# Two exponentials of the odd attention head side by side, with one shift of both row minima

## The chip, the core and the metric

The kernel runs on one core of a Trainium2 chip. A core has a matrix engine (TensorE, PE in the profile, with its weight loads shown apart as PEld), a vector engine (VectorE, DVE), an engine for activation functions (ScalarE, ACT), a general engine (GpSimd, POOL), and SyncE (SP), which here issues the transfers. Each engine works through its own list of instructions; semaphores make one wait for another. Matrix products go into PSUM, a small memory of banks, from which ACT and DVE read them. The metric is the device time of one run in microseconds (us).

## The reference

Two independent layers work on sequences of 2048 rows and 576 features, and their outputs stand side by side. The first is attention with a compressive memory: 32 heads of 18 features, in 4 segments of 512 rows.

```python
for s in range(N):
    qs, ks, vs = q[:, :, s], k[:, :, s], v[:, :, s]
    logits = jnp.einsum("bhqd,bhkd->bhqk", qs, ks) * scale + mask
    p = _softmax(logits, axis=-1)
    a_dot = jnp.einsum("bhqk,bhkd->bhqd", p, vs)
    ...
    o = g * a_mem + (1.0 - g) * a_dot
```

The mask is causal, so a block of 128 query rows needs 128, 256, 384 or 512 key columns. Ahead of the attention stand the projections of q, k and v, and behind it the output projection. The second layer is a Fourier mixing, `y = dft_seq_re @ a - dft_seq_im @ b` with `a` and `b` from two products over the features: large products with nothing to wait for but their operands.

## The kernel before

The program has three stretches: projections and memory sums; then attention, with the products of the Fourier layer ("dense work") as filler between its steps; then the rest of the dense work and the output projection. The edit touches the middle one, from about 245 to 905 us.

Its order is written out by hand. `attention()` is a generator that walks over pairs of heads, `p` from 0 to 67; each pair has eight slots, and after each slot it yields a weight. The driver (lines 1230 to 1239) then issues dense products until their share of the work has caught up. Operations given to `later` are issued so many slots after the call. Each engine gets its instructions in the order of this walk.

A pair of heads is in flight over several steps of `p`. The even head is worked with keys on the partitions (`t_fill`, banks with the tag `t`); the odd head with queries on the partitions (`f_fill`, `f_exp`), two steps later (`F_LAG = 2`). For the odd head:

- `f_fill(n, kind)` has PE compute scores into a PSUM bank (line 969), and DVE find each row's minimum of the negated, masked scores (`smallest`, line 975), into a column of the small tile `nb`. The four query blocks are dealt out to three banks by `ROWS`: kind 0 is the block with 512 columns (`nb` column 3), kind 1 those with 128 and 384 (columns 0 and 2), kind 2 the one with 256 (column 1). DVE's result appears in the profile as the row that reads its accumulator out.
- `f_exp(n, kind)` shifts these minima by a constant with an ACT copy (line 995), and then runs one exponential for each block of this kind on ACT (line 998), with the shifted minimum as its bias, from PSUM into the tile `pf`. After it the bank is free.
- `f_split_hi` (line 1005, ACT) and `f_split_lo` (line 1009, POOL and DVE) cut `pf` into a float16 pair `hl`; `f_turn` (line 1014) transposes that by a DMA from SP's queue, and `pv` (lines 1093 and 1094, PE) multiplies it by the values, a step later.

The banks: kinds 1 and 2 of the odd head share two banks, tag `s`, in turn with the three score steps `s_fill` of another even head (lines 969 and 975 again). `s_fill(n, 1)` in slot 1 takes the bank that kind 2 of the odd head used in slot 6 of the step before. Kind 0 goes to one of two `t` banks, which `t_fill(n, 1)` (line 1049, behind the small transpose of line 1026) takes next. In slot 4 the odd head's kind 0 takes this bank again, after DVE's `t_lo(n, 1)` (line 1076, `plo<-t`) has read the even head's exponentials, which line 1061 writes back into it.

Slots that matter, with what the edit touches: slot 3 to 4 has `f_fill` kinds 1 and 0; slot 6 has `pv` of another odd head, `f_fill` kind 2, `f_exp` kind 1; slot 7, the last, has `f_exp` kind 0 and `pv_out`; slot 0 of the next step has `t_lo`, `f_exp` kind 2 and `f_split_hi`; slot 1 has `s_fill` kinds 0 and 1 with `t_fill` kinds 0 and 1. Between slots, ACT also copies finished dense tiles out of PSUM (line 635 and line 652) and cuts the streamed DFT matrix into a high part (line 452), whose low part POOL makes (line 457).

Of the kernel before, what the change touches and what calls it, by code (L numbers as in the profile page):

```python
# [16 lines left out]
AF = mybir.ActivationFunctionType  # L17
# [6 lines left out]
P = 128  # L24
# [16 lines left out]
def infini_attention_and_fnet(ctx: ExitStack, tc: tile.TileContext, xT, wqk, w8, wv, wo, beta, xtT, cT, hT, out):  # L41
    nc = tc.nc
    act, dve, pool, pe = nc.scalar, nc.vector, nc.gpsimd, nc.tensor
# [44 lines left out]
    def later(n, fn, *a):  # L88
        due.setdefault(clock[0] + n, []).append((fn, a))
# [374 lines left out]
    def stacks(p_, i):  # L464
        qs_bufs.append(p_.tile([P, 4, L], BF16, name=f"qs{i}"))
        ks_bufs.append(p_.tile([P, 4, L], BF16, name=f"ks{i}"))
        pool.memset(ks_bufs[i].bitcast(F32)[96:], BF16_ONES)
# [20 lines left out]
    def stack_load(G):  # L488
        if G < NG:
            s, g8 = divmod(G, 8)  # L490
            rows = slice(g8 * 72, g8 * 72 + 72)
            for n, (buf, src) in enumerate(((ks_bufs, kd), (qs_bufs, qd))):
                later(1 + n, dma, buf[G % 4][:NPAIR], src[s][rows].rearrange("(h d) c t -> (d c) h t", d=DH))
# [71 lines left out]
    def bank(name, shape, dtype, tag):  # L565
        turns[tag] ^= 1
        return ps.tile(shape, dtype, name=name, tag=f"{tag}{turns[tag]}", bufs=1)
# [392 lines left out]
    ROWS = (((3, 0),), ((0, 384), (2, 0)), ((1, 0),))  # L960
    FIRST_COL = {3: 0, 2: 512, 0: 896, 1: 1024}
# [26 lines left out]
        smallest(o, kind, -SCALE, F_[n][0])  # L988
        F_[n][2][kind] = o

    def f_exp(n, kind):
        nb, f, o = F_[n]
        o = o.pop(kind)
        m = nb[:, (slice(3, 4), slice(0, 3, 2), slice(1, 2))[kind]]
        act.activation(m, m, AF.Copy, bias=LIFT)
        for i, c in ROWS[kind]:
            w = (i + 1) * P
            act.activation(f[:, FIRST_COL[i]:FIRST_COL[i] + w], o[:, c:c + w], AF.Exp, bias=nb[:, i:i + 1], scale=-1.0)  # L998

    def f_split_hi(n):  # L1000
        f = F_[n][1]
# [14 lines left out]
    def maxima(G):  # L1016
        m, b = NEGM[G % 2].rearrange("p (h n) -> p h n", h=2), MB[G % 2][:, :24].rearrange("p (h c n) -> p c h n", h=2, c=3)
        r = sa.tile([P, 2, 4], F32, name="negx", bufs=2)
        pool.tensor_copy(b[:, 0], m)
        pool.tensor_tensor(r, m, b[:, 0], OP.subtract)  # L1020
        pool.tensor_copy(b[:, 1], r)
        pool.tensor_tensor(b[:, 2], r, b[:, 1], OP.subtract)

    def maxima_transpose(G, o):
        t = o[:, 384:512]
        pe.matmul(t, MB[G % 2], ident16, start=True, stop=True)
        yield
        w = sa.tile([24, P], BF16, name="mt", bufs=2)
        act.activation(w, t[:24], AF.Copy)
        for h in range(2):  # L1030
            later(1, dma, qs_bufs[G % 4][NPAIR:NPAIR + 3, 2 * h].rearrange("c (n t) -> c n t", n=4), w[12 * h:12 * h + 12])
# [64 lines left out]
    def pv_out(n2):  # L1096
        G, hh = divmod(n2, 2)
        s, g8 = divmod(G, 8)
        o = PV.pop(n2)
        og = OG[G % 2]  # L1100
        h0 = 4 * g8 + 2 * hh
        w = o[:, 440:].rearrange("p (h i c) -> p h i c", h=2, c=1)
        b = o[:, :144].rearrange("p (h i d) -> p h i d", h=2, i=4)
        o = o[:, :440].rearrange("p (h i c) -> p h i c", h=2, i=4)
        a = sa.tile([P, 8, DH], F32, name="pa", bufs=2)
        dve.reciprocal(w, o[:, :, :, 54:])
        dve.tensor_tensor(w, w, g1[:, h0:h0 + 2, None, None].to_broadcast([P, 2, 4, 1]), OP.mult)
        dve.tensor_reduce(a, o[:, :, :, :54].rearrange("p h i (c d) -> p (h i) d c", c=3), axis=AX, op=OP.add)
        to = og[:, :, 36 * hh:36 * hh + 36].rearrange("p i (h d) -> p h i d", d=DH)
        a = a.rearrange("p (h i) d -> p h i d", h=2)  # L1110
        if s == 0:
            dve.tensor_tensor(to, a, w.to_broadcast([P, 2, 4, DH]), OP.mult)
        else:
            dve.tensor_tensor(b, a, w.to_broadcast([P, 2, 4, DH]), OP.mult)
            dve.tensor_tensor(to, to, b, OP.add)
        if hh == 1:
            later(6, turn_out, G)
# [33 lines left out]
    F_LAG, T_LAG, V_LAG = 2, 3, 4  # L1151
# [3 lines left out]
    def attention():  # L1155
        for p in range(NP + V_LAG):
            def even(lag, fn, *a):
                if 0 <= p - lag < NP:
                    fn(2 * (p - lag), *a)

            def odd(lag, fn, *a):
                if 0 <= p - lag < NP:
                    fn(2 * (p - lag) + 1, *a)

            if p < 2:
                OG.append(sa.tile([P, 4, 72], F32, name=f"og{p}"))
            if p == 0:
                stack_load(1)
                later(20, value_load, 0)
            if p % 2 == 0:  # L1170
                later(39, value_load, p // 2 + 1)
                later(30, memory_load, p // 2)
            even(T_LAG + 1, t_lo, 0)
            odd(F_LAG + 1, f_exp, 2)
            odd(F_LAG + 1, f_split_hi)
            yield SLOTS[0]
            G = p // 2 - 1 if p % 2 == 0 and 0 < p <= NP else None
            even(0, s_fill, 0)
            even(T_LAG, t_fill, 0)
            even(T_LAG, t_fill, 1, G)  # L1180
            even(0, s_fill, 1)
            if G is not None and p < T_LAG:
                list(maxima_transpose(G, bank("trm", [P, L], F32, "t")))
            odd(F_LAG + 1, f_split_lo, pool, 512, 1280)
            yield SLOTS[1]
            even(T_LAG, t_lo, 1)
            odd(F_LAG + 1, f_split_lo, dve, 0, 512)
            yield SLOTS[2]
            even(V_LAG, pv)
            if p < 2:  # L1190
                stacks(sq, p + 2)
            even(0, s_fill, 2)
            even(T_LAG, t_mask)
            yield SLOTS[3]
            odd(F_LAG, f_fill, 1)
            even(T_LAG, t_fill, 2)
            odd(F_LAG, f_fill, 0)
            if p % 2 and p < NP:
                maxima(p // 2)
            yield SLOTS[4]  # L1200
            odd(F_LAG + 1, f_turn)
            if p % 2:
                if p == 1:
                    later(6, stack_load, 2)
                else:
                    stack_load((p + 3) // 2)
                if 2 < p < 18:
                    later(2, copy_parts, 2, 7 + p // 2)
            elif 4 <= p < 36:
                later(2, copy_parts, 3, (p - 4) // 2)  # L1210
            even(T_LAG, t_hi)
            yield SLOTS[5]
            odd(V_LAG, pv)
            odd(F_LAG, f_fill, 2)
            odd(F_LAG, f_exp, 1)
            even(T_LAG, t_lo, 2)
            yield SLOTS[6]
            odd(F_LAG, f_exp, 0)
            if V_LAG <= p < NP + V_LAG - 1:
                pv_out(p - V_LAG)  # L1220
            yield SLOTS[7]
# [8 lines left out]
    for n, w in enumerate(attention()):  # L1230
        tick()
        ta += w
        for fn, a in PLAN.pop(n, ()):
            fn(*a)
        while td / total_d < ta / total_a:
            t = next(d, BREAK)
            if t is BREAK:
                break
            td += t
# [56 lines left out]
```

## Time and profile before

| | |
|---|---|
| median of 3 runs | 984.33 us (983.99 to 985.59) |
| the profiled execution's own time | 983.87 us |
| its span, first to last instruction | 982.2 us |
| granted PE clock, share of full | 0.999 |
| ACT copies of line 995 | x192, 38.0 us |
| ACT exponentials of line 998 | x256, 128.1 us |
| ACT halves of line 1005 | x128, 87.4 us |

The span is the time between the first and the last instruction of one profiled execution; that execution took 1.7 us longer in all. A row of the timeline gives the start, the duration, the engine, the line, the operation, the tile written and those read, shapes, and in brackets the idle time of the engine just before with what ended it. Rows of neighbours of one kind are merged (x2, x4). A table of stretches gives each engine's busy time between two moments; a table of waits says who waited for whom, in us, how often, and the longest. "PEld" rows are weight loads that run beside the products. A PE row's end is modelled, its start is not.

### The profile page before, as it was taken

How to read it: one execution, taken by the hardware profiler on the slowest of the kernel's cores; microseconds unless marked ns; L12 is line 12 of the kernel's file. 1: busy time of each engine (PE TensorE's matmuls, PEld its weight loads, DVE VectorE, ACT ScalarE, POOL GpSimd, SP SyncE). 2: the span in 40 equal slices, each digit the busy share in tenths (PEclk: the TensorE clock that was granted, in tenths of full speed). 3: DMA queues.
4: the chain of work that ended last, by engine and by line, in shares of the span. 5: the costliest groups of instructions: out<-in, count | busy, mean ns of one | idle time of the engine just before them, and what ended most of it. 6: DMA issues, size and time to landing. Idle time of an engine off the chain costs nothing.

```text
span 982.2 us, 25421 instructions
## 1 busy us (share of the span) xinstructions
PE 974.7 (99%) x9246; PEld 916.3 (93%) x9246; DVE 746.6 (76%) x2113; ACT 715.2 (73%) x1687; POOL 664.4 (68%) x746
## 2 busy tenths in 40 slices
PE   9999999999999999999999999999999999999998
PEld 8989989899999999999999999999999999999998
DVE  6657668594677767777887777778888899988884
ACT  6757576664887787877878788887777877878442
POOL 2657577686667766676776776667677987776561
PEclk9999999999999999999999999999999999999999
DMA  7637557766877998999999997789999999997663
GB/s 240 200 118 242 199 171 252 238 239 182 191 183 209 219 239 233 216 210 254 233 243 241 235 210 191 184 203 217 242 238 252 242 237 240 233 207 184 173 203 109
DMA packets 304350, 209.96 MB, mean 214 GB/s; under 512 B 204992, under 2 KB 259136, under 8 KB 304192
## 3 DMA queue, kind: packets, MB, share of 16 engines
q1 hardware_dynamic: 304000, 208.20, 82.5%
q8 instruction: 72, 1.18, 0.5%
q14 instruction: 54, 0.44, 0.1%
q10 hardware_dynamic: 224, 0.14, 0.0%
HBM read 122.37 MB, written 58.98 MB: 185 GB/s over the span
## 4 chain that ended last, share of the span: by engine, by line
PE 98%; ACT 1%; DVE 1%; issue 0%
PE d L584 41%; PE s L969 7%; PE v L84 6%; PE qk L84 6%; PE qk L251 6%; PE pv L1093 4%; PE d L629 3%; PE d L630 3%; PE d L631 3%; PE t L869 2%; PE pv L1094 2%; PE d L869 2%; PE s L869 2%; PE m L364 1%; PE t L1044 1%; PE look L397 1%
## 5 line engine op out<-in xcount | busy, mean ns | idle before, releaser
L975 DVE CUSTOM_DVE_ANT_0 s<-s,causal 128x128 f32<-128x128 f32 (+3 forms) x512 | 250.1, 504 | 104.3 <-PE s L969 98.1
L457 POOL TENSOR_TENSOR clo<-craw,chi 128x512 fp32r<-128x512 f32 x159 | 217.6, 1369 | 97.1 <-ACT chi L452 72.2
L584 PE MATMUL d<-wide,chi 128*128 128x288 f32 x1408 | 260.1, 302 | 0.0
L584 PEld LDWEIGHTS d<-wide,chi 128*128 128x128 f32 x1408 | 210.5, 188 | 0.7
L584 PE MATMUL d<-wide,clo 128*128 128x288 f32 x704 | 171.2, 310 | 0.0
L1009 POOL TENSOR_TENSOR hl<-pf,hl 128x768 f16<-128x768 f32 x64 | 113.9, 1780 | 70.3 <-ACT hl L1005 56.1
L969 PE MATMUL s<-ks,qs 108*128 108x128 bf16 (+3 forms) x512 | 131.6, 301 | 1.9 <-ACT pf L998 1.8
L1057 ACT ACTIVATE phi<-t 128x384 f16<-128x384 f32 x128 | 61.7, 482 | 98.1 <-PE t L1054 98.1
L998 ACT ACTIVATE pf<-s,nb 128x128 f32<-128x128 f32 (+3 forms) x256 | 128.1, 526 | 6.2
L584 PE MATMUL d<-ab,chi 128*128 128x288 f32 x640 | 122.3, 300 | 0.0
L584 PEld LDWEIGHTS d<-wide,clo 128*128 128x128 f32 x704 | 117.7, 188 | 0.9
L452 ACT ACTIVATE chi<-craw 128x512 fp32r<-128x512 f32 x160 | 99.6, 623 | 2.8 <-DMA craw<-xtT 1.8
L584 PEld LDWEIGHTS d<-ab,chi 128*128 128x128 f32 x640 | 97.6, 188 | 0.3
L1005 ACT ACTIVATE hl<-pf 128x768 f16<-128x768 f32 (+1 forms) x128 | 87.4, 729 | 2.0
L584 PE MATMUL d<-ab,clo 128*128 128x288 f32 x320 | 82.4, 306 | 0.0
L629 PE MATMUL d<-wide,chi 128*128 128x288 f32 x256 | 79.7, 311 | 0.0
L630 PE MATMUL d<-wide,chi 128*128 128x288 f32 x256 | 75.6, 295 | 0.0
L631 PE MATMUL d<-wide,clo 128*128 128x288 f32 x256 | 75.6, 295 | 0.0
L1061 ACT ACTIVATE pf<-t 128x512 f32<-128x512 f32 (+1 forms) x128 | 68.7, 537 | 7.4 <-PE t L1044 7.3
L1076 POOL TENSOR_TENSOR plo<-pf,phi 128x384 f16<-128x384 f32 x64 | 60.7, 948 | 15.1 <-ACT pf L1061 12.6
L969 PEld LDWEIGHTS <-qs 108*128 108x128 bf16 x512 | 44.4, 97 | 16.3 <-issue 2.7
L289 POOL TENSOR_TENSOR p<-r,p 128x512 bf16<-128x512 f32 x36 | 43.4, 1206 | 22.3 <-ACT p L288 21.1
(286 smaller groups left out, 2596.6 us busy)
## 6 DMA issues: line engine op xcount, KB each, us to landing
craw<-cT SPq DMA_DIRECT2D x128, 256.0 KB
ks<-kd SPq DMA_DIRECT2D x32, 432.0 KB
qs<-qd SPq DMA_DIRECT2D x32, 432.0 KB
craw<-xtT SPq DMA_DIRECT2D x32, 320.0 KB
vd<-vs SPq DMA_DIRECT2D x16, 440.0 KB
vst<-vd SPq DMA_DIRECT2D x32, 220.0 KB
qd<-p SPq DMA_DIRECT2D x16, 384.0 KB
kd<-p SPq DMA_DIRECT2D x16, 384.0 KB
```

What stands on the lines that cost most here:

```text
L84: pe.matmul(o, a, b, start=n == 0, stop=n == len(terms) - 1)
L452: act.activation(hi, raw[:, :4], AF.Copy)
L457: engine.tensor_tensor(lo, raw[:, :4], hi.bitcast(F32), OP.subtract)
L584: pe.matmul(o[h], a, b[:, h * 288:h * 288 + 288], start=start, stop=stop)
L629: pe.matmul(o, xh[:, k], wl[k][:, cs], start=k == 0, stop=False)
L630: pe.matmul(o, xh[:, k], wh[k][:, cs], start=False, stop=False)
L631: pe.matmul(o, xl[:, k], wh[k][:, cs], start=False, stop=False)
L969: pe.matmul(o[:, c:c + w], q[:, i * P:w], k[:, :w], start=True, stop=True)
L975: dve.tensor_tensor_reduce(o[:, c:c + w], o[:, c:c + w], CAUSAL[0][:, L - w:], scale=scale, scalar=-LOWEST, op0=OP.add, op1=OP.min, accum_ ...
L998: act.activation(f[:, FIRST_COL[i]:FIRST_COL[i] + w], o[:, c:c + w], AF.Exp, bias=nb[:, i:i + 1], scale=-1.0)
L1005: act.activation(hl[:, 0, a:b], f[:, a:b], AF.Copy)
L1009: engine.tensor_tensor(hl[:, 1, a:b], f[:, a:b], hl[:, 0, a:b], OP.subtract)
```

## The change

`f_exp` takes several kinds. It now shifts the minima of all of them with one copy over a strided slice of `nb`: columns 0 and 2 for kind 1, as before, and columns 1 and 3 for kinds 0 and 2 together. Then it runs the exponentials of the kinds in turn. Kind 2 leaves slot 0 of the following step; kinds 0 and 2 are done by one call in slot 7, the 512-column exponential first and the 256-column one behind it. The exponentials themselves, their operands and their banks stay as they are.

```diff
-    def f_exp(n, kind):
+    def f_exp(n, *kinds):
         nb, f, o = F_[n]
-        o = o.pop(kind)
-        m = nb[:, (slice(3, 4), slice(0, 3, 2), slice(1, 2))[kind]]
+        m = nb[:, 1 - kinds[0]::2]
         act.activation(m, m, AF.Copy, bias=LIFT)
-        for i, c in ROWS[kind]:
-            w = (i + 1) * P
-            act.activation(f[:, FIRST_COL[i]:FIRST_COL[i] + w], o[:, c:c + w], AF.Exp, bias=nb[:, i:i + 1], scale=-1.0)
+        for kind in kinds:
+            for i, c in ROWS[kind]:
+                w = (i + 1) * P
+                act.activation(f[:, FIRST_COL[i]:FIRST_COL[i] + w], o[kind][:, c:c + w], AF.Exp, bias=nb[:, i:i + 1],
+                               scale=-1.0)
+            del o[kind]
...
             even(T_LAG + 1, t_lo, 0)
-            odd(F_LAG + 1, f_exp, 2)
             odd(F_LAG + 1, f_split_hi)
             yield SLOTS[0]
...
             yield SLOTS[6]
-            odd(F_LAG, f_exp, 0)
+            odd(F_LAG, f_exp, 0, 2)
```

## The prediction

> **What bounds the kernel now.** First the page's first and fourth parts: busy time of each engine, and the chain that ended last.
>
> ```profile
> PE 974.7 (99%) x9246; PEld 916.3 (93%) x9246; DVE 746.6 (76%) x2113; ACT 715.2 (73%) x1687; POOL 664.4 (68%) x746
> PE 98%; ACT 1%; DVE 1%; issue 0%
> ```
>
> TensorE (PE) sets the end; the engine that the edit touches, ScalarE (ACT), has a quarter of its time free. So ACT's work counts only where PE waits for it. The second view is the table of stretches for the 660 us in which attention runs, the third the table of waits, cut to PE.
>
> ```profile
> 245.00:905.00 660.00, 658.04 (x7100) 621.28 (x7099) 527.15 (x1640) 527.11 (x1255) 468.40 (x524) 1.00 0.94 222
> PE s L969 <- ACT pf L998: 1.8, 4, 0.5
> ```
>
> Columns of the first row after the length: PE, PEld, DVE, ACT, POOL busy, clock, DMA share, GB/s. PE lacks 2 us of 660, and four waits for line 998, the exponentials of the odd head, are 1.8 us of them. A busy share can hide stalls, since ends of matmuls are modelled, so the starts are read in the timeline:
>
> ```profile
> 505.27 0.69 PE L584 MATMUL d<-wide,chi 128*128 128x288 f32 x4
> 505.79 0.43 PE L584 MATMUL d<-wide,clo 128*128 128x288 f32 x2
> ```
>
> Four products start in 0.52 us: 0.13 us each, closely packed. The Trainium skill (Perfetto Trace Analysis, Identifying the Most-Contended Engine) says that matmul busy time is a poor measure of the room left and that weight loading is a better one; by it some 7% would be open, and ACT's relief might buy more than four waits. The starts just quoted do not bear that out here.
>
> Fourth, the timeline at the first of the four waits:
>
> ```profile
> 257.92 0.69 ACT L998 ACTIVATE pf<-s,nb 128x512 f32<-128x512 f32 x1
> 258.54 0.41 ACT L635 ACTIVATE wide<-d 128x288 fp32r<-128x288 f32 x1
> 258.85 0.33 PE L1049 MATMUL t<-qs,ks 111*128 111x384 bf16 x1
> 259.07 0.47 ACT L998 ACTIVATE pf<-s,nb 128x256 f32<-128x256 f32 x1
> 259.60 0.38 PE L969 MATMUL s<-ks,qs 108*128 108x128 bf16 x2 [0.42 <-ACT pf L998]
> ```
>
> PE's score product at 259.60 needs the bank that the 256-column exponential frees at 259.54. That one stands behind an evacuation of a dense product (L635), emitted between the end of one pair and the start of the next. Its cost is read from starts: undisturbed, the score product follows L1049 after 0.16 us.
>
> ```profile
> 500.43 0.33 PE L1049 MATMUL t<-qs,ks 111*128 111x384 bf16 x1
> 500.59 0.38 PE L969 MATMUL s<-ks,qs 108*128 108x128 bf16 x2
> ...
> 283.57 0.33 PE L1049 MATMUL t<-qs,ks 111*128 111x384 bf16 x1
> 284.31 0.38 PE L969 MATMUL s<-ks,qs 108*128 108x128 bf16 x2 [0.42 <-ACT pf L998]
> ...
> 376.49 0.33 PE L1049 MATMUL t<-qs,ks 111*128 111x384 bf16 x1
> 377.30 0.38 PE L969 MATMUL s<-ks,qs 108*128 108x128 bf16 x2 [0.48 <-ACT pf L998]
> ...
> 447.71 0.33 PE L1049 MATMUL t<-qs,ks 111*128 111x384 bf16 x1
> 448.55 0.38 PE L969 MATMUL s<-ks,qs 108*128 108x128 bf16 x2 [0.51 <-ACT pf L998]
> ```
>
> The four distances are 0.75, 0.74, 0.81 and 0.84 us; less 0.16 each that is 0.59 + 0.58 + 0.65 + 0.68 = 2.50 us, all that PE loses to the banks of these exponentials (more than the 1.8 us of the waits, which count only from L1049's modelled end).
>
> **The change part by part.** *Removed:* one shift copy in each of 64 pairs, 0.20 us each (the row at 506.94 below), so 64 x 0.2 = 12.8 us of ACT. It lies under PE's work and is worth nothing in itself; without that cover it would be worth those 12.8 us.
>
> *Moved:* the 256-column exponential now starts right behind the 512-column one. Nothing is issued with it, no DMA moves, and PE's order stays as it is. At the other place in the loop, in an undisturbed pair:
>
> ```profile
> 506.94 0.20 ACT L995 ACTIVATE nb<-nb 128x1 f32<-128x1 f32 x1
> 507.17 0.69 ACT L998 ACTIVATE pf<-s,nb 128x512 f32<-128x512 f32 x1
> 507.25 0.14 DVE L975 DVE_READ_ACCUMULATOR2_ANT nb<- 128x1 f32 x1
> 507.76 0.62 ACT L452 ACTIVATE chi<-craw 128x512 fp32r<-128x512 f32 x1
> 508.50 0.47 ACT L998 ACTIVATE pf<-s,nb 128x256 f32<-128x256 f32 x1
> ```
>
> The next ACT instruction starts 0.59 us after a 512-column exponential (507.17 to 507.76), and the 256-column one takes 0.47: 1.06 us from the start of the first to the end of the second. In the four stalled pairs this ends at 257.92 + 1.06 = 258.98, against PE's undisturbed 259.01: the stall goes.
>
> ```profile
> 282.45 0.69 ACT L998 ACTIVATE pf<-s,nb 128x512 f32<-128x512 f32 x1
> 374.13 0.69 ACT L998 ACTIVATE pf<-s,nb 128x512 f32<-128x512 f32 x1
> 446.92 0.69 ACT L998 ACTIVATE pf<-s,nb 128x512 f32<-128x512 f32 x1
> ```
>
> Likewise 283.51 against 283.73 (gone); 375.19, even with a hold of 0.5 us as worked out below, against 376.65 (gone); and 447.98 against 447.87, which leaves 0.11 and some 0.05 for the release (ACT ended at 259.54, PE went at 259.60). With 0.03 left at the first, 2.50 - 0.16 - 0.03 = **2.3 us gained**.
>
> *Added:* the copy now waits for the 256-column minimum too. In the pair above that is read out at 507.25 + 0.14 = 507.39, so the copy starts near 507.42 in place of 506.94: ACT, which works in order, is held 0.48 us, and behind the copy stand the 512-column exponential, the cut of the next DFT chunk (L452), and the float16 halves (L1005). The second exponential still ends at 507.42 + 0.23 + 1.06 = 508.71, before its old 508.97. Read in this way in all 64 pairs the hold runs from none (the first pair) over 0.7 us (the last) to 1.54 us:
>
> ```profile
> 245.72 0.14 DVE L975 DVE_READ_ACCUMULATOR2_ANT nb<- 128x1 f32 x1
> 245.95 0.19 ACT L995 ACTIVATE nb<-nb 128x1 f32<-128x1 f32 x1
> ...
> 852.76 0.20 ACT L995 ACTIVATE nb<-nb 128x1 f32<-128x1 f32 x1
> 854.13 0.14 DVE L975 DVE_READ_ACCUMULATOR2_ANT nb<- 128x1 f32 x1
> ...
> 903.12 0.20 ACT L995 ACTIVATE nb<-nb 128x1 f32<-128x1 f32 x1
> 903.68 0.14 DVE L975 DVE_READ_ACCUMULATOR2_ANT nb<- 128x1 f32 x1
> ```
>
> Who waits behind it on PE? In the worst pair (852.76) the 512-column exponential ends at 854.30 + 0.24 + 0.69 = 855.23 and the 256-column one at 855.60; PE asks for their banks some 0.8 us later:
>
> ```profile
> 856.43 0.33 PE L1049 MATMUL t<-qs,ks 111*128 111x384 bf16 x1
> 856.59 0.38 PE L969 MATMUL s<-ks,qs 108*128 108x128 bf16 x2
> ...
> 857.49 0.50 ACT L1061 ACTIVATE t<-t 128x384 f32<-128x384 f32 x1
> 858.57 0.54 DVE L1076 TENSOR_TENSOR plo<-t,phi 128x384 f16<-128x384 f32 x1
> 860.51 0.38 PE L969 MATMUL s<-ks,qs 108*128 108x512 bf16 x1
> ```
>
> What is late next is the even head's chain: ACT's third exponential (L1061 into t), VectorE's (DVE's) difference (L1076), and the bank that PE needs for the odd head's 512 columns (L969). The hold moves ACT by about 1.3 us here (1.54, less the saved copy), the exponential's end from 857.99 to 859.3 and the difference to 859.9; PE comes at 860.51, so 0.6 us remain even here. After that ACT stands idle in any case until PE's next even scores, which takes the lateness away before the next pair:
>
> ```profile
> ACT phi L1057 <- PE t L1054: 98.1, 60, 3.0
> ```
>
> That is 1.6 us in 60 of the pairs. So the hold costs nothing; uncovered it would cost up to 1.5 us a pair. The bounds of this unknown: no cost at one end, at the other what the third rival works out.
>
> The sum is made on the profiled execution, 983.87 us (span 982.2 and 1.7 around it): 983.87 - 2.3 = 981.6. The median of the runs, 984.33, lies 0.46 above it; on that the forecast is 982.0 us.
>
> **The rivals.** *Forecast, 982.0: the four stalls go and the holds are covered.* For it: every stall in the attention stage has the one cause named, and all margins read stay positive.
>
> *Rival 1, part given back, 983.6.* The reductions come later than the rows say, or the lateness adds up with DVE's own work. With 0.6 us more of hold in every pair, the sum done above for the worst pair gives seven pairs in which the difference L1076 frees the bank too late, 1.6 us together: 984.33 - 2.3 + 1.6. For it: 0.6 us is all the margin that the pair with the longest hold has left, and pairs with shorter holds can have less. Against it: the typical hold, about half a microsecond, would have to double.
>
> *Rival 2, no effect, 984.3.* The two waits for banks only change places: the copy's wait costs at the early stalls what the order saves. Against it: at each of the four the exponential's new end, worked out above, still lies half a microsecond or more ahead of the old one.
>
> *Rival 3, slower, 988.4.* The hold at the copy decides: from about 1 us beyond the rows, the difference L1076 comes too late in about 19 of the pairs (margins of 0.3 to 1.6 us used up), 6.4 us together: 984.33 - 2.3 + 6.4. It begins to outweigh the gain above 0.7 us. For it: two of the three holds quoted are 0.7 and 1.54 us already. Against it: ACT's idle 1.6 us a pair, part of which comes before the difference. A page's rule works the same way: by the Trainium skill (SBUF — State Buffer, Who interferes with whom) a DVE instruction with two SBUF inputs contends with GpSimd reads, so later POOL work could fall onto DVE's; what that would cost no row of before shows apart.
>
> **How the numbers follow.** Chances: forecast 0.54, rival 1 0.22, rival 2 0.08, rival 3 0.16. A measurement of this kernel tells about 0.2% (2 us) from no change. The forecast is 0.24% and so just beyond it: faster 0.54; rivals 1 and 2 within 0.2%: 0.30; slower 0.16. The range goes from 981.2 (2.5 us gained, and 0.6 for scatter: the lowest of the runs, 983.99, lies 0.34 below the median) to 985.5 (a hold of 0.8 us more, 3.5 us given back); it leaves out most of rival 3.
>
> **What would show it.** Right: PE's waits for line 998 gone, the score product 0.16 us after L1049 at the four places, PE busy all but 0.5 us of 245 to 905; ACT's wait for the minimum (L975) at line 995 risen to some 20 to 35 us (64 holds of about 0.5 us, partly hidden), and its wait for L1054 fallen by as much, less the saved copies; the copies 128 in number. Wrong: a new wait of PE, for DVE's L1076 or for line 998, or more than 0.2 us between undisturbed L1049 and score product.

## The result, and the profile after

| | before | after |
|---|---|---|
| median of 22 runs each | 984.57 us (983.71 to 985.59) | 982.64 us (981.44 to 985.77) |
| profiled execution, and its span | 983.87 us, span 982.2 us | 981.44 us, span 979.7 us |
| ACT copies of the shift | x192 | x128 |

The ratio of the times is 0.9985, with a 95% interval from 0.9979 to 0.9992: the kernel became faster by 0.15%, or 1.5 us (0.8 to 2.1); the means are 1.4 us apart. The gain is sure, but it lies under the 0.2% that the prediction had named as the line; the two profiled executions are 2.4 us apart, the medians 1.9. The profiled execution after is the fastest of its 22 runs, 1.2 us under their median; the one before lies 0.7 us under its own.

The page after, busy times and the chain that ended last:

```profile
PE 974.2 (99%) x9246; PEld 916.4 (94%) x9246; DVE 742.1 (76%) x2113; ACT 702.2 (72%) x1623; POOL 661.4 (68%) x746
PE 99%; ACT 0%; DVE 0%; issue 0%
```

PE's work is the same (9246 products, half a microsecond less busy), ACT has 13.0 us less. The table of stretches for the attention stage, and the whole table of waits of PE:

```profile
245.00:905.00 660.00, 659.94 (x7121) 623.66 (x7120) 525.18 (x1643) 515.87 (x1194) 466.09 (x525) 1.00 0.94 223
PE warm L240 <- DVE ones L68: 1.1, 1, 1.1
```

PE lacks 0.06 us of 660 where it had lacked 1.96, and it did 21 more products in the stretch. The waits for line 998 are gone. At the first of the four places the timeline now reads

```profile
256.87 0.14 DVE L975 DVE_READ_ACCUMULATOR2_ANT nb<- 128x1 f32 x1
257.82 0.19 ACT L994 ACTIVATE nb<-nb 128x2 f32<-128x2 f32 x1
258.05 1.05 ACT L998 ACTIVATE pf<-s,nb 128x512 f32<-128x512 f32 x2
258.98 0.33 PE L1051 MATMUL t<-qs,ks 111*128 111x384 bf16 x1
258.99 0.41 ACT L635 ACTIVATE wide<-d 128x288 fp32r<-128x288 f32 x1
259.15 0.38 PE L969 MATMUL s<-ks,qs 108*128 108x128 bf16 x2
```

One copy of two columns, both exponentials in 1.05 us (the prediction had put 1.06), and the evacuation L635 behind them. (Lines 994, 1046, 1051, 1056, 1059, 1063 and 1078 after are 995, 1044, 1049, 1054, 1057, 1061 and 1076 before.) The score product follows L1051 (formerly L1049) after 0.17 us instead of 0.75. The last of the four keeps a rest:

```profile
446.05 0.33 PE L1051 MATMUL t<-qs,ks 111*128 111x384 bf16 x1
446.36 0.38 PE L969 MATMUL s<-ks,qs 108*128 108x128 bf16 x2
```

That is 0.31 us, 0.15 above an undisturbed one. Both traces hold PE's 9246 products in the same order, so their starts can be set against each other one by one. The difference of start times after minus before moves by -0.58 us at the first stall, then by -0.57, -0.63 and -0.52 at the other three, and by -0.22 at 758.9 us of the trace before; 0.12 is lost among the first products of the program, and it ends at -2.42. These are differences of single starts, taken from the traces.

ACT's own waits after, the groups that changed:

```profile
ACT phi L1059 <- PE t L1056: 90.7, 59, 2.5
ACT nb L994 <- DVE nb L975: 28.6, 42, 1.4
ACT pf L1063 <- PE t L1046: 1.4, 5, 0.4
```

The hold for the second minimum is there, 28.6 us in 42 of the pairs and up to 1.4 us in one, and no product waits for it. Before, ACT waited 1.5 us for minima, so the hold adds 27.1. It is paid with the 12.8 us of copies that went and with idle time that ACT spent on PE anyway: 98.1 to 90.7 us before the even scores of slot 4, 7.3 to 1.4 before those of slot 1, which makes 26.1 together.

### The profile page after: what moved, and what is told of

Its sections match the earlier page's. It is cut to its first block, busy times and chain, and to the rows that moved or that the text cites. A ratio compares the mean times of both kernels' runs of the same rounds, so it can differ in the third digit from the quotient of the medians.

```text
span 979.7 us, 25347 instructions
## 1 busy us (share of the span) xinstructions
PE 974.2 (99%) x9246; PEld 916.4 (94%) x9246; DVE 742.1 (76%) x2113; ACT 702.2 (72%) x1623; POOL 661.4 (68%) x746
## 4 chain that ended last, share of the span: by engine, by line
PE 99%; ACT 0%; DVE 0%; issue 0%
PE d L584 42%; PE s L969 7%; PE v L84 6%; PE qk L84 6%; PE qk L251 6%; PE pv L1095 4%; PE d L629 4%; PE d L630 3%; PE d L631 3%; PE pv L1096 2%; PE t L869 2%; PE d L869 2%; PE s L869 2%; PE t L1046 1%; PE m L364 1%; PE look L397 1%
## 5 line engine op out<-in xcount | busy, mean ns | idle before, releaser
L1011 POOL TENSOR_TENSOR hl<-pf,hl 128x768 f16<-128x768 f32 x64 | 107.7, 1683 | 66.7 <-ACT hl L1007 54.2
L1059 ACT ACTIVATE phi<-t 128x384 f16<-128x384 f32 x128 | 61.9, 483 | 90.9 <-PE t L1056 90.7
L998 ACT ACTIVATE pf<-s,nb 128x128 f32<-128x128 f32 (+3 forms) x256 | 121.0, 524 | 4.2
L452 ACT ACTIVATE chi<-craw 128x512 fp32r<-128x512 f32 x160 | 100.0, 625 | 2.8 <-DMA craw<-cT 1.2
```

What stands on the lines that cost most here:

```text
L452: act.activation(hi, raw[:, :4], AF.Copy)
L998: act.activation(f[:, FIRST_COL[i]:FIRST_COL[i] + w], o[kind][:, c:c + w], AF.Exp, bias=nb[:, i:i + 1], scale=-1.0)
L1011: engine.tensor_tensor(hl[:, 1, a:b], f[:, a:b], hl[:, 0, a:b], OP.subtract)
```

## The experiments

**Order alone, and shift alone.** The change has two parts. The first kernel moves the 256-column exponential and leaves each kind its own copy:

```diff
-            odd(F_LAG + 1, f_exp, 2)
...
             odd(F_LAG, f_exp, 0)
+            odd(F_LAG, f_exp, 2)
```

> The place of the 256-column exponential alone, each kind with its own shift copy again (192 copies). My theory (only the four waits of TensorE for the 256-column exponential's bank cost time): they go here too, so 0.15% to 0.25% under the kernel before, 982.2 to 983.1 us, with no wait of TensorE for the exponentials over 0.3 us, and ScalarE's wait for the minima a few us in place of 28.6. Rival (the single shift, 64 copies of 0.2 us less, is what is worth the time): as the kernel before, 984.5 us.

Measured: median 982.45 us (981.85 to 983.0), ratio 0.9976 (0.9967 to 0.9986). PE's one wait for an exponential:

```profile
PE s L969 <- ACT pf L998: 0.2, 1, 0.2
```

ACT waits 3.0 us for the minima instead of 28.6. By the times, the order alone brings the whole gain. By the starts of the products it brings 1.8 us of the 2.3 at the four places: against the trace of the whole change, the second copy between the exponentials gives back 0.24 us at the first, 0.03 at the second and 0.22 at the last. So the single shift is worth about half a microsecond on top of the order, too little to be seen in the times.

The second kernel does the reverse, with one copy for columns 1 and 3 in the last slot and the exponential in slot 0 as before:

```diff
-        m = nb[:, (slice(3, 4), slice(0, 3, 2), slice(1, 2))[kind]]
-        act.activation(m, m, AF.Copy, bias=LIFT)
+        if kind < 2:
+            m = nb[:, 1 - kind::2]
+            act.activation(m, m, AF.Copy, bias=LIFT)
```

> The single shift copy alone: columns 1 and 3 in the last slot, the 256-column exponential in slot 0 as before (128 copies). My theory: ScalarE is held for the 256-column minimum some 30 us in all, which is covered, and the four waits of TensorE stay, though each about 0.2 us shorter, as the copy ahead of that exponential is gone: 0.05% to 0.12% under the kernel before, 983.4 to 984.1 us, with TensorE waits of 1 to 2 us for the exponentials. Rival (the copies saved are the gain): 982.6 us as with the whole change. Rival (the hold costs): over 985 us.

Measured: median 984.17 us (983.23 to 987.41), ratio 0.9999 (0.9989 to 1.0009): nothing that the times can tell, where 0.05% to 0.12% had been expected. Its waits of PE and of ACT:

```profile
PE s L969 <- ACT pf L999: 0.9, 4, 0.3
ACT nb L996 <- DVE nb L975: 27.8, 41, 1.4
```

The four waits stay, halved: by the starts PE gains 0.23 us at each place. The hold of 27.8 us stands alone here, with no better order beside it, and no product of PE waits for it. PE loses 0.31 us at one more place, at 479.2 us, but there the 256-column exponential stood behind a cut of the DFT matrix (L452) for which ACT had waited 0.90 us, on a transfer. So the saved copies are not what the change gained, and the hold is covered; the times alone, good to some 1 us here, would leave room for a small cost.

**How much hold the cover bears.** In the third kernel each exponential of the last slot is done twice, in the fourth (run later) only the 256-column one. The results stay the same:

```diff
-            for i, c in ROWS[kind]:
+            for i, c in ROWS[kind] * (1 if kind == 1 else 2):
```

> The changed kernel with each exponential of the last slot done twice (same results, about 1.0 us more of ScalarE in each of 64 pairs), as a hold 1 us longer than the change brings. My theory (cover of about 1 us a pair, read from the margins in the changed kernel's trace): some 20 pairs overrun, 5 us of TensorE waits in all (3 to 8), 987.6 us (985.6 to 990). Rival (ScalarE's idle time of 130 us in this stage covers it all): 982.6 us. Rival (every pair pays the whole microsecond): 1046 us.

> The changed kernel with the 256-column exponential alone done twice: 0.5 us more of ScalarE a pair ahead of the bank that TensorE's next score product takes, none ahead of the other bank. My theory (most margins are 0.9 to 1.8 us, so half a microsecond overruns few pairs): 1.3 us of waits by the margins of the changed kernel's trace, up to 2.5, so 0.1% to 0.3% over the changed kernel, 984 to 986 us, at three to six places. Rival (cover of the same size is lacking in all pairs alike, in proportion to what doubling both did: 14.7 us for 1.2 us more): 6 us more, 988.5 us.

Measured: both twice, 997.29 us (996.76 to 997.64), ratio 1.0126 (1.0112 to 1.014), so about 14 us over the changed kernel; the 256 columns twice, 984.12 us (983.35 to 985.08), ratio 0.9993 (0.9984 to 1.0002). PE's waits with both done twice:

```profile
PE s L969 <- ACT pf L998: 4.1, 12, 0.5
PE t L1028 <- ACT pf L998: 1.4, 3, 0.8
PE s L969 <- DVE plo L1078: 1.1, 3, 0.6
PE d L584 <- ACT y L652: 0.6, 1, 0.6
```

and a pair of it in the timeline:

```profile
325.86 2.28 ACT L998 ACTIVATE pf<-s,nb 128x512 f32<-128x512 f32 x4
327.77 0.33 PE L1051 MATMUL t<-qs,ks 111*128 111x384 bf16 x1
328.19 0.38 PE L969 MATMUL s<-ks,qs 108*128 108x128 bf16 x2
```

The expectation of 5 us fell. One cause is the dose: the four exponentials take 2.28 us against 1.05 for two, so 1.23 us were added and not 1.0. And most waits are for the exponentials' own banks (the 0.42 us above, where 0.16 is undisturbed), not for DVE's difference behind them. By the margins of the changed kernel's trace a hold of 1.2 us overruns 27 pairs, for 8 us at the 256-column bank and 4 at the difference, some of it twice; the measured 14 is above that, and the rest is not accounted for. With the 256 columns alone twice, PE lost 1.5 us at four places (0.51, 0.31, 0.50, 0.17) to the exponentials, as expected: half a microsecond ahead of one bank is mostly covered, while 1.2 us, which also holds the 512-column bank, cost about ten times as much.

**Why the runs of the changed kernel scatter.** Its fastest run is 2.3 us under the fastest before, its longest no better than the longest before. So the changed kernel was run again, eleven times on each of two chips and in two single profiled executions, and the order alone again on the second of these chips:

> The changed kernel once more, for a second profile and the scatter of its runs (981.4 to 985.8 us so far, against 983.7 to 985.6 before). My theory: the median stays 0.15% under the kernel before; a profile of a slower execution shows the same four waits gone and its lost 2 to 4 us at one other place, in a wait that the faster profile lacks. Rival: the four waits come back in the slower executions.

> The order alone, repeated beside the changed kernel on one chip. Theory A (the wait for the second minimum makes the time depend on how an execution falls out, so that some executions of the changed kernel give 1 to 4 us back): runs of this kernel stay within 981.8 to 983.2 us, the changed kernel's scatter to 986. Theory B (the scatter is the chip's own): both scatter alike.

> The changed kernel beside the run of the order alone. Theory A: median 0.05% or more over the order alone, runs from 981.3 to 986 us. Theory B: the same distribution as the order alone, within 0.05%.

> A look at one more execution of the changed kernel. Theory A: if it takes more than 983 us, TensorE waits 1 us or more in the attention stage for something released by ScalarE (an exponential's bank, or VectorE's difference behind it). Theory B: if it takes more than 983 us, the time is lost outside the attention stage, or all over in transfers.

> The same look again, for an execution that falls out otherwise: as for the look before.

Measured: the changed kernel 983.2 us (981.25 to 986.21; ratio 0.9984, 0.9973 to 0.9995) and 983.91 (981.57 to 988.31; ratio 0.999, 0.9976 to 1.0003), single executions of 981.28 and 983.24; the order alone 983.5 (982.08 to 984.62; ratio 0.9983, 0.9974 to 0.9992). So the order alone scatters too, if less far, and the tie to the shared shift is not shown. On both chips its median was the lower one, by 0.75 and 0.41 us, with intervals that overlap: that the single shift helps is not shown either. In none of the five profiles of the changed kernel did the four waits come back; set against the trace before, each of the five gains 0.57 to 0.58, 0.57, 0.63 and 0.52 us at the four places. What differs lies elsewhere: the program's first products take up to 0.7 us more in one of them, and the gain of 0.22 at 758.9 is absent in another. The profiles reach from 981.28 to 983.24 us; none of the longer runs, up to 988.31, left one. In the execution of 983.24 us the table of PE's waits has one entry more:

```profile
PE d L584 <- ACT y L652: 1.0, 1, 1.0
```

and, in its timeline,

```profile
495.81 0.63 ACT L452 ACTIVATE chi<-craw 128x512 fp32r<-128x512 f32 x1 [2.33 <-DMA craw<-cT]
496.35 0.19 ACT L994 ACTIVATE nb<-nb 128x2 f32<-128x2 f32 x1
497.54 1.05 ACT L998 ACTIVATE pf<-s,nb 128x512 f32<-128x512 f32 x2
500.41 0.69 ACT L652 ACTIVATE y<-d 128x288 f32<-128x288 f32 x2
500.85 0.53 PE L584 MATMUL d<-wide,chi 128*128 128x288 f32 x2 [1.04 <-ACT y L652]
```

A chunk of the DFT matrix landed late. ACT, in whose queue its cut stood first, was idle for 2.33 us, and everything behind it came late: the odd head's exponentials, and the evacuation that frees PE's dense bank. By the starts this place cost 1.5 us of the 1.8 between this execution and the first one. The second profile of the order alone has the same wait of 1.0 us at the same place, behind 2.26 us of ACT's waiting for the chunk.

Issue and cut of this chunk in the kernel before, in the changed kernel's first trace, and its issue in the slower execution:

```profile
487.80 0.41 SPq L442 DMA_DIRECT2D craw<-cT  x1
495.54 0.63 ACT L452 ACTIVATE chi<-craw 128x512 fp32r<-128x512 f32 x1
...
487.96 0.68 SPq L442 DMA_DIRECT2D craw<-cT  x1
493.98 0.63 ACT L452 ACTIVATE chi<-craw 128x512 fp32r<-128x512 f32 x1 [0.52 <-DMA craw<-cT]
...
487.98 0.42 SPq L442 DMA_DIRECT2D craw<-cT  x1
```

SP issues the load at the same time in all three, but ACT comes to the cut 7.74 us after the issue in the kernel before and 5.50 us after it in the changed one (493.98 - 0.52 - 487.96). In the slower execution ACT could start the cut 7.83 us after the issue (495.81 - 487.98): by these numbers that would have cost ACT some 0.1 us before the change, an estimate. At this place the gain has used up the room that the transfer had.

**Loads earlier.** To try that cause, the chunks' loads were issued some 2 us earlier, in the changed kernel, in the kernel before, and with the order alone:

```diff
-        c_load(n + 4)
+        later(2, c_load, n + 5)
```

> The changed kernel with each streamed DFT chunk's load issued some 2 us earlier (two slots into the use of the chunk five ahead of it, in place of the start of the one four ahead). My theory (the scatter of the changed kernel's runs, 981.3 to 988.3 us, comes from such loads landing late, which holds ScalarE's queue and, behind it, the copy that frees a dense bank): runs within 981 to 983 us, median 981.3 to 982.3, no wait of ScalarE for a chunk over 0.5 us. Rival (the scatter has another source, or the earlier loads collide with other transfers): runs scatter to 984 us and over as before.

> The same earlier loads in the kernel before. My theory (the four waits are there in every execution and are worth 2.4 us, late loads come on top): runs within 983.3 to 985 us, median 983.5 to 984.5, and 2.0 to 2.5 us over the changed kernel with the same loads. Rival (the order of the exponentials only shifts how late loads strike): less than 1 us between the two.

> The order alone (each kind with its own shift copy) together with the earlier loads of the DFT chunks. My theory (the four waits gone are worth 2.4 us, late chunk loads are one of two sources of scatter, late transfers of the row minima's transposed copy the other, and the single shift is worth 0.5 us at most): fastest run 981.3 to 982.0 us, median 982 to 983.2, any TensorE wait over 0.5 us is for a transfer. Rival (the single shift is needed with it): median over 983.5 us, as the kernel before with the same loads (983.71).

| | median | runs | ratio to before |
|---|---|---|---|
| earlier loads, changed kernel | 982.49 | 980.96 to 987.14 | 0.998 (0.9966 to 0.9995) |
| earlier loads, kernel before | 983.71 | 983.35 to 985.05 | 0.9991 (0.9982 to 1.0) |
| earlier loads, order alone | 982.08 | 981.52 to 983.02 | 0.9971 (0.9961 to 0.9982) |

The medians of the first two are 1.22 us apart, less than the 2.0 to 2.5 expected and more than the rival's 1; their fastest runs are 2.39 apart. By the starts in the two profiles, the four places are worth 0.56, 0.56, 0.64 and 0.54 us, 2.3 together, on top of the earlier loads too. But the first row still scatters, and its profile shows a second source:

```profile
473.87 0.72 SPq L94 DMA_DIRECT2D qs<-mt  x1
479.06 0.40 PE L1046 MATMUL t<-qs,ks 111*128 111x128 bf16 x4 [1.70 <-DMA qs<-mt]
```

PE waited 1.7 us for the transposed row maxima. The row is the second of two issues of that copy, 5.2 us ahead; the same issue stands at 471.57 in the changed kernel's first trace, 2.3 us sooner, while PE would have come at the same time in both (477.35). So the copy was issued late: ahead of it in SP's list the issue of `qs<-qd` took 2.23 us, against 0.45 in the first trace. Whether the earlier loads brought that about is not shown. The expectation that late chunk loads explain all of the scatter fell, and one wait of 0.6 us for a chunk was left in the stage. The last row has the lowest median of the study, where it was expected, with no run over 983.02 us; its interval overlaps that of the order alone (0.9967 to 0.9986), whose first ten runs went no higher than 983.0 us either. Whether the earlier loads or the separate copies hold its runs together was not taken apart further.

## Why the prediction was right

- *The bound and the stalls.* PE sets the end, and only its waits count: the span fell by 2.4 us, PE's missing time in the stage by 1.9. That the busy share hid no more was borne out: the start times in the two traces differ at the stalls, at 758.9 us and at the program's start, and nowhere else. So the caution of the Trainium skill (Perfetto Trace Analysis, Identifying the Most-Contended Engine) changed nothing in the account here.
- *The term of the sum.* 2.3 us from the four waits, measured 0.58 + 0.57 + 0.63 + 0.52 = 2.30 between the two traces, and the same in the four other profiles of the changed kernel. The forecast of 0.16 us left at the last place met 0.15. Not foreseen were the 0.22 us at 758.9, where in the trace of before DVE was late (its difference L1076 took 2.01 us at 755.26, and 1.78 after). They are no part of the change: the kernel before with the earlier loads did not lose them, and one execution of the changed kernel did.
- *The hold.* Forecast some 20 to 35 us in all, up to 1.5 us in a pair and free; measured 28.6, up to 1.4, and free, shown by the shift alone. That ACT's wait for L1054 would fall by as much less the copies, some 16 us, was right in kind only: it fell by 7.4, and another 5.9 came from the wait ahead of slot 1.
- *The place of the time, 982.0 against a measured 982.64.* The likeliest case, more than 0.2% faster, was missed by little; the term that was mis-sized is the step from one execution to the median, for which the prediction carried over the 0.46 us of before and which was 1.2 us after. In the traces the four places give 2.3 us; over 22 runs 1.5 (0.8 to 2.1) are left. That lies midway between the forecast and the 0.7 us that rival 1 leaves, but not by rival 1's mechanism: in no trace of the changed kernel does a product of this stage wait for the reductions or for DVE's work. The one changed execution over 983 us that was profiled lost its time to a late load in ACT's queue; the late copy of the maxima was seen only in kernels that had been altered further. Why the changed kernel's runs reach further up from their fastest than those before is open in part: for one chunk the traces show that ACT now comes 2.2 us sooner to a load that is issued no sooner, but no run isolates that, and none of the longest runs was profiled.
- *Rival 3.* Its point of onset was about right (half a microsecond costs 1.5 us, 1.2 cost 14), but its price was too low (6.4 us for a hold of about 1) and its place wrong: the bank of the 256-column exponential gives way first, not the difference at L1076.

## What to carry to other kernels

Where one engine works without a break, look up its few waits one by one and ask what stands ahead of the releasing instruction in its queue; putting the release ahead of work that has to wait anyway was worth all of the gain that the times could tell here (1.8 us of 2.3 in the traces), and saving 12.8 us of ACT's copies was worth nothing that they could tell. A merged wait (one copy for two minima) may cost nothing while the engine has idle time behind it; measure how much, since the cost beyond the cover rose from 1.5 us with 0.5 us of added hold ahead of one bank to 14 with 1.2 ahead of two. A consumer that comes sooner leaves less room to a transfer that is not issued sooner: look at the time from issue to use before and after. When the gain in one trace is larger than in the medians, compare several traces product by product before doubting the mechanism.

## What the runs showed that was not expected

- Exponentials repeated into the same columns did not overlap: 2.28 us for four against 1.05 for two, where the single rows sum to 2.32 and 1.16. The Trainium skill (ScalarE: Activation LUTs, What ACT_TABLE_LOAD costs) has neighbours overlap by about 93 ns. The 512-column and the 256-column one agree with it (0.10 us); a repeat starts 0.03 us after the one before it has ended. In the trace each repeat first waits for a semaphore that ACT's own instructions raise, and the 256-column one behind the 512-column one does not.
- A single transfer that lands late, of a chunk (2.33 us of ACT, 1.5 of PE) or of the row maxima (1.70 us of PE), moves a run of this kernel by as much as the change moved the runs (1.5 us), in a stage where the DMA engines are busy 94% of the time.
